# State products in fp32, longer turns and a new order of steps in an attention and softplus kernel on one Trainium2 core

## The chip, the core and the metric

The kernel runs on one core of a Trainium2 chip. Five engines work side by side, each through a queue of its own in order: PE (matrix products, with its weight loads PEld), DVE and ACT (element-wise work; both can read PSUM, where the products land), POOL (element-wise work, in SBUF alone) and SP (issues DMA transfers here). The metric is the device time of one execution in microseconds. The profiled execution has a span, from its first to its last instruction; the time is a little longer than the span.

## The reference

Attention runs both ways between 512 tokens and 32 state rows of each head; then every row of both results goes through a two-layer network with softplus.

```
B, H, S, Ns, D = (8, 8, 512, 32, 64);  d_model, d_ff = 512, 2048
scores  = scale * x @ state^T;  a  = softmax over the state rows;  xread = a @ state
scores2 = scale * state @ x^T;  a2 = softmax over the tokens;      sread = a2 @ x
x = concatenate([xread, sread], axis=2), heads joined to 512 features
h = x @ w_in;  g = max(h, 0) + log1p(exp(-|h|));  out = g @ w_out
```

The two weight matrices come in as 64-bit floats, x and state as 32-bit ones. Products on PE run in one of two ways. An fp32 product takes both operands whole. A split product has its operands as two parts, high and low (F32R), and runs as passes high-high, high-low, low-high.

## The kernel before

**What is computed.** For the token rows, `xread @ w_in` is not done as two products: V = state . w_in is made per head once, and the first layer is `a @ V`. A slot is 128 hidden features of one batch: six products on L454 (`gemm1`), then the softplus on ACT (L438 to L440) and DVE (L441), the split of its result (`ghi` by ACT or POOL, `glo` by DVE or POOL, L85 to L93), and twelve products on L461 (`gemm2`) into four PSUM banks called acc, one for each 128 tokens. There are 16 slots for each of the eight batches, and eight slots of 256 features for the rows of the state read. The banks are: h, two; aux, two; acc, four.

**Stages.** A string of letters sets the order. START covers the whole attention of batches 0 to 2 and the slots of batches 0 and 1; BLOCK runs once for each of the batches 2 to 6; then come the state read and LAST with batch 7. The letters: `|` a slot's first product and softplus, `g` the second product of the oldest slot that waits, `a b c` a step of a batch's attention, `v V U` a step of making V, `W` one 128-row piece of w_out, `F` and `p` the fetch and the split of a piece of V. The set MOVED says which splits and copies go to POOL or DVE.

**Making V.** A 128-row piece of w_in is loaded (`load_w`, L98) and converted from 64 bits to 32 (`as_f32`): an ACT or POOL product with 2^-112 (L114, L112) and three DVE instructions (L124, L125, L126). Six of the pieces take another way (L118 to L122, two DVE instructions and one each on ACT and POOL). The first 512 hidden features (chunk 0, `make_v0`) use fp32 products with the padded state, `QZ` (L167 for batches 0 and 1, kept in SBUF as `vf`; L176 for batches 2 and 3, sent to DRAM). For chunks 1 to 3 `make_v` splits each piece again by head: `head` (L213 to L219) makes the 64 rows of one head into a high and a low half, in the tile `zhl`; `product` (L202 to L211) multiplies them by the state of four batches, `StK`, which lies in the room of two w_out tiles; the result goes through `ve` to DRAM (`Vd`) and comes back by `fetch_v` (L260) for each batch. Batches 4 to 7 are made likewise during the BLOCKs from weights kept in DRAM (`wsc`), in the tile `R`.

**Turns.** Batches 0 and 1 take turns by quarters of the hidden features, eight turns of four slots. At a turn's end the four acc banks go to SBUF: the first time by ACT copies (L549), later by DVE additions (L552).

**Rows of a group** in PE's order: `QZ` and `zhl` stand for the fp32 state products' weights, `zhl,wout` for a head's split products. Two products of 64 columns on L424 end batch 2's attention; the second of them is the last step of START on PE.

Of the kernel before, what the change touches and what calls it, by code (L numbers as in the profile page):

```python
# [12 lines left out]
I64 = mybir.dt.int64  # L13
AF = mybir.ActivationFunctionType
# [5 lines left out]
P = 128  # L20
# [12 lines left out]
RTAGS = ('zhl',)  # L33
VLAG = (2, 2)
V_ORDER = (1, 2, 3)
LOADS = (('t', 0), ('w', 0), ('w', 0), ('w', 0), ('z', 0), ('x', 0), ('q', 1), ('q', 0), ('w', 0), ('w', 0), ('w', 0), ('t', 1), ('w', 0), ('x', 1), ('w', 0))
ATT = (('Q0', 'A0', 'M0', 'Q1', 'N0', 'A1', 'M1', 'D0', 'E0', 'N1', 'E1', 'D1', 'G0', 'R0', 'G1', 'R1', 'X0', 'X1'), ('Q0', 'A0', 'M0', 'N0', 'Q1', 'D0', 'A1', 'M1', 'N1', 'D1', 'E0', 'G0', 'R0', 'X0', 'E1', 'G1', 'R1', 'X1'), ('Y0', 'S0', 'Q0', 'E0', 'A0', 'G0', 'M0', 'N0', 'D0', 'S1', 'R0', 'X0', 'Q1', 'A1', 'E1', 'M1', 'N1', 'G1', 'Y1', 'R1', 'D1', 'X1'), ('S0', 'Q0', 'E0', 'Y0', 'G0', 'A0', 'S1', 'R0', 'M0', 'X0', 'Y1', 'N0', 'Q1', 'A1', 'M1', 'E1', 'G1', 'N1', 'R1', 'X1', 'D1', 'D0'))
START = 'aaagvavavaBavaaavaaaaaaapabvWaWva|vVVVVVbWbV|pbVb|bVbbVbgbgW|VVVgpbb|V|VVbpgVVWbV|bWgbF|gWVWVpbbg|gVp|gVVVV||FgbVpVVV||VVWgVgWVpVVV|WVVg|gVFVWVVggp|V|VVVVVVpggF|gCVp|cg||WgpFcWgpWWcpF||gg|c||cF|cgcccgcpgcpc|g|cccccc|gg|cpcccgc'
BLOCK = 'UBUg|UU|gbpUU|bbgbbU|Fgpbbp|UbUgUbbFU|gUFU|bbUbFbgb|pU|gpbUgUbb|UUUgbpUUgUUp||UUUgUbbpbg|U|gUUU|gb|g'
LAST = 'pFg||gpF|Fggg||pgp|gg||gp|pg||ggg|gp|g|g||'  # L40
# [648 lines left out]
```

## Time and profile before

| | |
|---|---|
| time, median of 3 runs | 726.08 us (726.03 to 726.4) |
| span of the profiled execution | 723.7 us |
| PE busy | 669.6 us |
| DVE busy | 526.1 us |
| ACT busy | 484.9 us |
| POOL busy | 217.2 us |
| data moved | 89.76 MB |

Busy times of PE overlap: a product's record runs from its start to its end, and the next one starts before that end. The stretch between two starts is what a product costs when they follow each other. An fp32 product shows as two records in the trace, and as one row in the order of instructions.

### The profile page before, as it was taken

To read this page: it belongs to the slowest core of one execution; us is meant where nothing else is said; L and a number is where in the kernel's file an instruction comes from. 1 tells how busy PE (TensorE), PEld (TensorE's weight loads), DVE (VectorE), ACT (ScalarE), POOL (GpSimd) and SP (SyncE) were. 2 spreads that over 40 slices of the span, in tenths; PEclk is the share of its full clock that TensorE was granted. 3 is DMA by queue.
4 is the path that set the end of the run, shared out by engine and by line. 5 is a ranking of instruction groups with operands and counts; after the bars stand their busy time and mean duration, and the time that the engine had idled before them with its cause. 6 is when DMAs were issued, how large, how long until landed. Compare 5 with 4: busy or idle time off the path is not lost.

```text
span 723.7 us, 9466 instructions
## 1 busy us (share of the span) xinstructions
PE 669.6 (93%) x3012; PEld 538.4 (74%) x3012; DVE 526.1 (73%) x881; ACT 484.9 (67%) x897; POOL 217.2 (30%) x218
## 2 busy tenths in 40 slices
PE   3777869799799999999999999999999999999997
PEld 1445657577687787887888888888888889988886
DVE  4889888999999999569874975498558744534322
ACT  3565868576767787778786776667666676656653
POOL 2456466645754421022110411141113101012100
PEclk9999999999999999999999999999999999999999
DMA  8777727565632645436442421141112112522001
GB/s 293 232 230 246 242 92 257 171 211 163 191 95 95 209 140 178 124 102 203 153 131 88 145 59 59 30 146 30 29 30 87 30 30 73 161 87 60 1 0 59
DMA packets 46194, 89.76 MB, mean 124 GB/s; under 512 B 6976, under 2 KB 13888, under 8 KB 46144
## 3 DMA queue, kind: packets, MB, share of 16 engines
q1 hardware_dynamic: 46144, 89.15, 38.7%
q8 instruction: 24, 0.39, 0.2%
q14 instruction: 26, 0.21, 0.1%
HBM read 60.29 MB, written 28.84 MB: 123 GB/s over the span
## 4 chain that ended last, share of the span: by engine, by line
PE 56%; DVE 26%; ACT 5%; issue 5%; DMA 2%; POOL 2%; SPq 0%; DVEq 0%; ACTq 0%; POOLq 0%
PE acc L461 33%; PE h L454 15%; PE h L501 3%; DVE t L441 3%; DVE glo L93 2%; DVE k L93 2%; PE aux L204 2%; DVE zhl L219 2%; DVE wt L126 2%; DVE k L125 2%; DVE vhl L93 2%; DVE k L124 1%; DVE k L328 1%; PE aux L387 1%; ACT t L438 1%
## 5 line engine op out<-in xcount | busy, mean ns | idle before, releaser
L461 PE MATMUL acc<-wout,ghi 128*128 128x512 f32 x1088 | 339.7, 393 | 3.5 <-DVE o L144 1.0
L461 PEld LDWEIGHTS acc<-wout,ghi 128*128 128x128 f32 x1088 | 203.0, 189 | 48.1 <-DVE o L144 2.0
L461 PE MATMUL acc<-wout,glo 128*128 128x512 f32 x544 | 212.4, 391 | 0.8 <-DVE glo L93 0.8
L454 PE MATMUL h<-aT,vhl 128*128 128x512 f32 x768 | 198.4, 397 | 12.2 <-DVE t L441 9.7
L454 PEld LDWEIGHTS h<-aT,vhl 128*128 128x128 f32 x768 | 144.1, 190 | 46.1 <-DVE t L441 9.8
L441 DVE SCALAR_TENSOR_TENSOR t<-h,t 128x512 f32<-128x512 f32 x136 | 93.2, 686 | 91.9 <-ACT t L440 91.2
L438 ACT ACTIVATE t<-h 128x512 f32<-128x512 f32 x136 | 80.8, 595 | 90.6 <-PE h L454 80.0
L461 PEld LDWEIGHTS acc<-wout,glo 128*128 128x128 f32 x544 | 102.5, 188 | 23.1 <-DVE glo L93 1.4
L93 DVE TENSOR_TENSOR glo<-t,ghi 128x512 fp32r<-128x512 f32 x98 | 75.0, 765 | 36.1 <-ACT ghi L92 21.0
L85 POOL TENSOR_SCALAR ghi<-t 128x512 fp32r<-128x512 f32 x51 | 34.5, 676 | 221.8 <-DVE t L441 189.9
L440 ACT ACTIVATE t<-t 128x512 f32<-128x512 f32 x136 | 85.6, 631 | 2.4
L439 ACT ACTIVATE t<-t 128x512 f32<-128x512 f32 x136 | 85.7, 632 | 1.4
L92 ACT CAST ghi<-t 128x512 fp32r<-128x512 f32 x85 | 52.7, 620 | 48.3 <-DVE t L441 37.4
L93 POOL TENSOR_TENSOR glo<-t,ghi 128x512 fp32r<-128x512 f32 x38 | 51.5, 1357 | 103.1 <-ACT ghi L92 93.1
L93 DVE TENSOR_TENSOR vhl<-vf,vhl 128x512 fp32r<-128x512 f32 x70 | 55.3, 792 | 29.7 <-ACT vhl L92 29.2
L92 ACT CAST vhl<-vf 128x512 fp32r<-128x512 f32 x69 | 42.2, 613 | 13.9 <-PE h L501 8.6
L209 ACT COPY ve<-aux 128x512 f32<-128x512 f32 x41 | 23.2, 579 | 3.5 <-PE aux L204 1.9
L204 PE MATMUL aux<-zhl,wout 128*128 128x512 f32 x48 | 16.1, 420 | 10.0 <-DVE ve L207 4.1
L501 PEld LDWEIGHTS h<-sreadT,vhl 128*128 128x128 f32 x192 | 24.1, 191 | 0.6
L501 PE MATMUL h<-sreadT,vhl 128*128 128x256 f32 x192 | 24.3, 283 | 0.0
L219 DVE TENSOR_TENSOR R<-wt,R 64x512 fp32r<-64x512 f32 x32 | 22.5, 704 | 2.4 <-ACT R L218 1.4
L126 DVE SCALAR_TENSOR_TENSOR wt<-k,k 128x512 int32<-128x512 int32 (+1 forms) x30 | 21.9, 730 | 2.2 <-POOL wout L93 1.2
(139 smaller groups left out, 745.9 us busy)
## 6 DMA issues: line engine op xcount, KB each, us to landing
vd<-ve SPq DMA_DIRECT2D x56, 256.0 KB, 2.3
vf<-vd SPq DMA_DIRECT2D x112, 128.0 KB, 2.8
xT<-in_xt_dram SPq DMA_DIRECT2D x16, 512.0 KB, 4.5
x<-in_xn_dram SPq DMA_DIRECT2D x16, 512.0 KB, 3.9
k<-in_w_out_dram SPq DMA_DIRECT2D x16, 512.0 KB, 3.8
k<-in_w_in_dram SPq DMA_DIRECT2D x12, 512.0 KB, 4.3
out_dram<-o SPq DMA_DIRECT2D x24, 256.0 KB, 2.1
wt<-wsc SPq DMA_DIRECT2D x16, 256.0 KB, 3.1
```

The source lines that it names most:

```text
L85: nc.gpsimd.tensor_scalar(dst, src, 1.0, 0.0, ALU.mult, ALU.add)
L92: nc.scalar.copy(hi, src)
L93: vec(*what).tensor_tensor(lo, src, f32(hi), ALU.subtract)
L126: nc.vector.scalar_tensor_tensor(r.bitcast(I32), h2.bitcast(I32), 3, u, ALU.logical_shift_left, ALU.bitwise_or)
L219: vec("R", *what, o).tensor_tensor(r[z], wf[a], f32(r[a]), ALU.subtract)
L438: nc.scalar.activation(t, h, AF.Abs)
L439: nc.scalar.activation(t, t, AF.Exp, scale=-1.0)
L440: nc.scalar.activation(t, t, AF.Ln, bias=1.0)
L441: nc.vector.scalar_tensor_tensor(t, h, 0.0, t, ALU.max, ALU.add)
L454: nc.tensor.matmul(h, Vhl[b, ft // 2][:, vi, g, cs], aT[b][:, ai, g], start=(n == 0), stop=(n == 5))
L461: nc.tensor.matmul(acc[c], g[gi][:, c0:c0 + P], wout[ft][:, wi], start=(ft == first and i == 0), stop=(ft == last and i == 2))
L501: nc.tensor.matmul(h[:, 256 * i:256 * i + 256], Whl[u, i][:, wi, kt, :], sreadT[:, si, kt, :], start=(n == 0), stop=(n == 11))
```

## The change

It does the following.

- Chunks 1 to 3 of V for batches 0 to 3 are made as chunk 0 is (`make_vf` in place of `make_v` for the first four batches): two fp32 products of a whole 128-row piece, 128x512, in place of two heads of two split products each. The first product's two halves are copied to SBUF as V of batches 0 and 1, in the room of the w_out tiles 10, 11, 13 and 14 (chunk 3: `vf`), and are not sent to DRAM; the second product holds batches 2 and 3 and goes to DRAM in one transfer a piece. The head splits, `StK` of the first four batches and 24 fetches fall away.
- Turns: five in place of eight, (batch 0, quarter 0), (1, 0-1), (0, 1-2), (1, 2-3), (0, 3).
- The weights of w_in and w_out can be issued ahead of their conversion, by the new letters `i` and `o`. The first eight pieces of w_in have rooms of their own (`k4`, `R`, `o`). The loads of x move from the batch's load to two steps `L` of its attention.
- The conversion's two DVE instructions on 32-bit words (mask the sign, shift and merge) become two on 16-bit halves, which write every second half word; the third stays. All pieces take this way, and its first product is always on ACT.
- START and LAST are new, BLOCK becomes three strings, and MOVED is new: 175 instructions on POOL, where there were 223.

```diff
-        nc.vector.tensor_scalar(u, hi, SIGN, None, ALU.bitwise_and)
-        nc.vector.scalar_tensor_tensor(u, lo, 29, u, ALU.logical_shift_right, ALU.bitwise_or)
+        uh = u.bitcast(U16).rearrange("p (n t) -> p n t", t=2)
+        nc.vector.tensor_scalar(uh[:, :, 0], vh[:, :, 1], 13, None, ALU.logical_shift_right)
+        nc.vector.tensor_scalar(uh[:, :, 1], vh[:, :, 3], 0x8000, None, ALU.bitwise_and)
...
+    VTAGS = {1: ("wout10", "wout11"), 2: ("wout13", "wout14"), 3: ("vf", "vf")}
...
+    def load_ahead(k):
+        if coming[k]:
+            come[k].append(load_w(coming[k].pop(0)))
...
+    def make_vf(cs):
+        for c in cs:
+            for b in range(2):
+                Vf[b, c] = sb(VTAGS[c][b], [P, 2, 512], bufs=2 if c == 3 else 1)
+            for q in range(4):
+                wf = as_f32(ahead("in"), c, q, tag="wout12" if (4 * c + q) % 3 == 2 else "wt")
+                nc.sync.dma_start(wsc[c][P * q:P * q + P, :], wf)
...
+                nc.tensor.matmul(pb, QZ[0][:, q, :], wf, start=True, stop=True)
...
+                for b in range(2):
+                    dst, src = Vf[b, c][r, q // 2], pb[64 * b:64 * b + 64]
...
+                nc.tensor.matmul(pb, QZ[1][:, q, :], wf, start=True, stop=True)
...
+                nc.sync.dma_start(Vd[0, c][:, q, :], ve)
...
+            if what == "L":
+                load_x(b, g)
...
-    slots = [(b, ft) for f0 in range(0, NFT, QTR) for b in (0, 1) for ft in range(f0, f0 + QTR)]
+    turns = [(0, 0, 1), (1, 0, 2), (0, 1, 3), (1, 2, 4), (0, 3, 4)]
+    slots = [(b, ft) for b, q0, q1 in turns for ft in range(QTR * q0, QTR * q1)]
...
-        run(BLOCK, b)
+        run({2: BLOCK2, 3: BLOCK3}.get(b, BLOCK), b)
```

On PE, in START, where a piece of chunk 1 is multiplied (`acc` rows are second products, `h` rows first products, `aux` rows the work on V and attention). Before:

```order
L461 MATMUL acc_555<-wout_130_451,glo_519 128x512
L454 MATMUL h_675<-aT_302,vhl_631 128x512 x3
L204 MATMUL aux_697<-zhl_601,wout_114_411 128x512
L204 MATMUL aux_697<-zhl_601,wout_115_412 128x512
L461 MATMUL acc_556<-wout_130_451,ghi_518 128x512 x2
L461 MATMUL acc_556<-wout_130_451,glo_519 128x512
L381 MATMUL aux_703<-x_198,a2T_647 128x256 x4
L204 MATMUL aux_723<-zhl_602,wout_114_411 128x512
L204 MATMUL aux_723<-zhl_602,wout_115_412 128x512
```

In the changed kernel the same place reads as follows (L215 and L226 are the two fp32 products of a piece, L493 and L500 the slots').

```order
L215 MATMUL aux_428<-wt_417,QZ_87 128x512
L500 MATMUL acc_583<-wout_74_283,ghi_387 128x512
L500 MATMUL acc_583<-wout_74_283,glo_388 128x512
L500 MATMUL acc_584<-wout_74_283,ghi_387 128x512 x2
L500 MATMUL acc_584<-wout_74_283,glo_388 128x512
L500 MATMUL acc_585<-wout_74_283,ghi_387 128x512
L226 MATMUL aux_444<-wt_417,wout_2_88 128x512
L493 MATMUL h_544<-aT_113,vhl_471 128x512 x4
L500 MATMUL acc_585<-wout_74_283,ghi_387 128x512
L215 MATMUL aux_462<-wout_133_457,QZ_87 128x512
```

A piece's two heads, of two rows each, have become two rows, whose operand is the converted piece itself, and they stand among the same slots' products.

On DVE, in START, at the conversion of one piece. Before, with the two head splits (L219) that follow it:

```order
L124 TENSOR_SCALAR k_193_669<-k_191_665 128x512
L358 RECIPROCAL rs_774<-rs_774 128x1
L125 SCALAR_TENSOR_TENSOR k_193_669<-k_191_665,k_193_669 128x512
L126 SCALAR_TENSOR_TENSOR wt_670<-k_192_667,k_193_669 128x512
L93 TENSOR_TENSOR wout_166_573<-wt_579,wout_166_573 128x512
L219 TENSOR_TENSOR zhl_691<-wt_670,zhl_691 64x512
L441 SCALAR_TENSOR_TENSOR t_656<-h_649,t_656 128x512
L219 TENSOR_TENSOR zhl_692<-wt_670,zhl_692 64x512
```

In the changed kernel, two conversions (a piece of w_in, `k_118`, and one of w_out, `k_126`), in START after the first softplus:

```order
L127 TENSOR_SCALAR k_118_416<-k_107_391 128x512
L129 SCALAR_TENSOR_TENSOR wt_398<-k_109_395,k_110_397 128x256
L128 TENSOR_SCALAR k_118_416<-k_107_391 128x512
L127 TENSOR_SCALAR k_126_437<-k_90_328 128x512
L129 SCALAR_TENSOR_TENSOR wt_417<-k_117_414,k_118_416 128x512
L128 TENSOR_SCALAR k_126_437<-k_90_328 128x512
L380 TENSOR_REDUCE sm_449<-T_393 128x16
```

One of the two instructions with two inputs has become one with a single input, and no split stands between the conversion and the product of `wt_417`.

On SP, at the start of the program, the loads in the order of their issue. Before:

```order
L274 DMA xT_90<-in_xt_dram 128x1024
L98 DMA k_4_92<-in_w_in_dram 128x256
L98 DMA k_5_94<-in_w_in_dram 128x256
L98 DMA k_6_96<-in_w_in_dram 128x256
L286 DMA Z_73<-in_zp_dram 128x2x64 x2
L279 DMA x_100<-in_xn_dram 128x1024
L616 DMA zhl_89<-in_zq_dram 128x512
L616 DMA QZ_88<-in_zq_dram 128x512
```

In the changed kernel:

```order
L310 DMA xT_89<-in_xt_dram 128x1024
L322 DMA Z_73<-in_zp_dram 128x2x64 x2
L98 DMA k_4_93<-in_w_in_dram 128x256
L98 DMA k_5_95<-in_w_in_dram 128x256
L310 DMA xT_97<-in_xt_dram 128x1024
L98 DMA k_7_99<-in_w_in_dram 128x256
L98 DMA k_8_101<-in_w_in_dram 128x256
L98 DMA R_103<-in_w_in_dram 128x256
```

The scores' operands (xT, Z) of both groups now stand ahead of most weights, and x has left this place; it is issued after the first three writes to `wsc`.

## Rows read from the trace of the kernel before

**Rows 1.** The page: busy time by engine, and the span in 40 slices.

```profile
PE 669.6 (93%) x3012; PEld 538.4 (74%) x3012; DVE 526.1 (73%) x881; ACT 484.9 (67%) x897; POOL 217.2 (30%) x218
...
PE   3777869799799999999999999999999999999997
...
DVE  4889888999999999569874975498558744534322
```

**Rows 2.** Windows: busy us (and records) by engine, granted clock, DMA share, GB/s.

```profile
0.00:40.00 40.00, 21.66 (x69) 13.26 (x69) 27.95 (x65) 16.85 (x40) 15.02 (x24) 0.93 0.80 260
40.00:229.50 189.50, 161.69 (x673) 122.97 (x671) 174.14 (x259) 129.88 (x245) 108.47 (x95) 0.98 0.56 182
229.50:310.00 80.50, 78.52 (x352) 63.25 (x352) 67.73 (x119) 64.74 (x120) 19.95 (x19) 1.00 0.50 159
310.00:390.00 80.00, 78.93 (x357) 64.21 (x356) 63.88 (x110) 62.98 (x116) 15.66 (x17) 1.00 0.45 143
390.00:461.00 71.00, 70.68 (x323) 58.15 (x323) 48.73 (x89) 49.08 (x90) 15.32 (x17) 1.00 0.27 79
```

**Rows 3.** Waits of PE, 40 to 229.5 us: total, times, longest.

```profile
PE h L454 <- DVE t L441: 9.7, 4, 3.9
PE aux L204 <- DVE ve L207: 4.1, 4, 1.6
PE aux L204 <- POOL zhl L219: 2.6, 4, 0.8
PE aux L204 <- DVE zhl L219: 1.6, 2, 0.8
```

**Rows 4.** Timeline of PE: start, duration; first slot, fp32 products, START's last step.

```profile
30.04 1.89 PE L381 MATMUL acc<-x,a2T 128*128 128x256 f32 x8
...
39.91 2.48 PE L454 MATMUL h<-aT,vhl 128*128 128x512 f32 x6
...
51.50 1.88 PE L317 MATMUL aux<-xT,Z 128*128 128x512 f32 x4
...
229.45 0.27 PE L424 MATMUL aux<-ident,sr 64*128 64x64 f32 x1
```

**Rows 5.** The chain of waits, one of its pieces: start, us, twelve products.

```profile
294.98 2.72 PE acc L461 x12
```

**Rows 6.** Groups of 0 to 229.5 us: busy us, mean ns, idle before.

```profile
L125 DVE SCALAR_TENSOR_TENSOR k<-k,k 128x512 int32<-128x512 int32 x24 | 19.8, 826 | 0.3
L126 DVE SCALAR_TENSOR_TENSOR wt<-k,k 128x512 int32<-128x512 int32 x24 | 19.5, 811 | 2.2 <-POOL wout L93 1.2 <-issue 0.5 <-DVE k L125 0.2
L219 DVE TENSOR_TENSOR zhl<-wt,zhl 64x512 fp32r<-64x512 f32 x16 | 17.3, 1083 | 2.3 <-ACT zhl L218 1.3 <-POOL zhl L85 0.5
L93 DVE TENSOR_TENSOR glo<-t,ghi 128x512 fp32r<-128x512 f32 x14 | 16.1, 1150 | 1.0 <-POOL ghi L85 0.5 <-ACT ghi L92 0.4
L124 DVE TENSOR_SCALAR k<-k 128x512 int32<-128x512 int32 x24 | 14.8, 617 | 0.1
L552 DVE TENSOR_TENSOR StK<-acc,StK 128x512 f32<-128x512 f32 x12 | 7.8, 673 | 0.0
```

**Rows 7.** Groups of 229.5 to 724 us, the same split later in the program.

```profile
L93 DVE TENSOR_TENSOR glo<-t,ghi 128x512 fp32r<-128x512 f32 x84 | 58.9, 701 | 35.1 <-ACT ghi L92 20.7 <-POOL ghi L85 13.3
```

**Rows 8.** Timeline of DVE and POOL: the same instructions alone and beside POOL.

```profile
31.01 0.42 DVE L124 TENSOR_SCALAR k<-k 128x512 int32<-128x512 int32 x1
...
31.94 0.69 DVE L125 SCALAR_TENSOR_TENSOR k<-k,k 128x512 int32<-128x512 int32 x1
...
100.36 1.64 POOL L93 TENSOR_TENSOR wout<-wt,wout 128x512 fp32r<-128x512 f32 x1
...
100.86 1.42 DVE L124 TENSOR_SCALAR k<-k 128x512 int32<-128x512 int32 x1
```

**Rows 9.** DMA issues: count, size, median us to landing.

```profile
k<-in_w_in_dram SPq DMA_DIRECT2D x12, 512.0 KB, 4.3
```

More of the change, by code (lines that the diff above doesn't have):

```diff
@@ L13 @@
 I64 = mybir.dt.int64
+U16 = mybir.dt.uint16
 AF = mybir.ActivationFunctionType
@@ L163, in make_v0 @@
             for q in range(4):
-                wt = as_f32(first.pop(0), 0, half, q)
+                k = 4 * half + q
+                wt = as_f32(first.pop(0), 0, half, q, tag=f"wout{4 + k}" if k < 6 else "wt")
                 nc.sync.dma_start(wsc[0][P * q:P * q + P, cs], wt)
@@ L181, in make_v0 @@
                     nc.scalar.copy(ve, pb[:, 0:256])
-                nc.sync.dma_start(Vd0[:, q, cs], ve)
+                nc.sync.dma_start(Vd[0, 0][:, q, cs], ve)
                 made["v0", half] = q
                 yield
-    StK = {}
-    def prep_stk(g4, tags):
-        if len(tags) > 1:
-            k = [sb(tag, [P, H, P], F32R) for tag in tags]
-        else:
-            t = sb(tags[0], [P, 2, H, P], F32R)
-            k = [t[:, 0], t[:, 1]]
-        StK[g4] = k
+    coming = {"in": [w_in[c, q] for c in range(1, 4) for q in range(4)],
+              "out": [w_out[P * ft:P * ft + P, :] for ft in range(NFT)]}
@@ new lines, in attention_then_softplus_mlp, with ahead @@
+    come = {"in": [], "out": []}
+    def load_ahead(k):
+        if coming[k]:
+            come[k].append(load_w(coming[k].pop(0)))
+    def ahead(k):
+        if not come[k]:
+            load_ahead(k)
+        return come[k].pop(0)
+    def make_vf(cs):
[5 more added lines that the diff above has]
+                nc.sync.dma_start(wsc[c][P * q:P * q + P, :], wf)
+                yield
+                pb = aux()
+                nc.tensor.matmul(pb, QZ[0][:, q, :], wf, start=True, stop=True)
+                r = slice(64 * (q % 2), 64 * (q % 2) + 64)
+                for b in range(2):
+                    dst, src = Vf[b, c][r, q // 2], pb[64 * b:64 * b + 64]
+                    if ("vd", c, q, b) in MOVED:
+                        nc.vector.tensor_copy(dst, src)
+                    else:
+                        nc.scalar.copy(dst, src)
+                made["v", c] = q
+                yield
+                pb = aux()
+                nc.tensor.matmul(pb, QZ[1][:, q, :], wf, start=True, stop=True)
+                ve = sb("ve", [P, 512], bufs=2)
+                if ("ve", 0, c, 2 * q + 1) in MOVED:
+                    nc.vector.tensor_copy(ve, pb)
+                else:
+                    nc.scalar.copy(ve, pb)
+                nc.sync.dma_start(Vd[0, c][:, q, :], ve)
+                made[0, c] = q
+                yield
@@ L430, in split_wout @@
     def split_wout(ft):
-        assert ft < NFT - 2 or all(made[0, c] == H for c in range(1, 4))
+        assert ft < NFT - 1 or all(made[0, c] == 3 for c in range(1, 4))
         wout[ft] = sb(f"wout{ft}", [P, 2, DM], F32R)
-        w = as_f32(load_w(w_out[P * ft:P * ft + P, :]), ft)
+        w = as_f32(ahead("out"), ft)
         split(wout[ft][:, 0], wout[ft][:, 1], w, "wout", ft)
@@ L455, in gemm1 @@
                 n += 1
-        return softplus(h, b, ft)
+        return softplus(h, min(b, 4), ft)
     def gemm2(acc, g, ft, cols, first=0, last=NFT - 1):
@@ L531, in flush @@
             return
-        first = ft // QTR * QTR if b < 2 else 0
-        last = first + QTR - 1 if b < 2 else NFT - 1
+        first, last = next(r for r in runs.get(b, [(0, NFT - 1)]) if r[0] <= ft <= r[1])
         if ft == first:
@@ L554, in flush @@
                     nc.sync.dma_start(d, p)
-    fetches = [(fetch_w, (ft,)) if b == B else (fetch_v, (b, ft // 4)) for b, ft in slots if b == B or ft % 4 == 0][2:]
+    fetches = [(fetch_w, (ft,)) if b == B else (fetch_v, (b, ft // 4)) for b, ft in slots if b == B or ft % 4 == 0 and b > 1]
     pieces = [(split_w, (ft,)) if b == B else (split_v, (b, ft // 2)) for b, ft in slots if b == B or ft % 2 == 0]
-    wt_tags = [f"wout{NFT - 2 + i}" for i in range(2)]
     first = []
@@ L597, in run @@
                     break
+            elif what in "io":
+                load_ahead({"i": "in", "o": "out"}[what])
             elif what == "g":
@@ L618, in attention_then_softplus_mlp @@
             load_z(0)
-        elif what == "t":
+        else:
             load_xT(0, i)
-        else:
-            load_x(0, i)
     run(START)
```

100 lines of the change are left out of this document (47 added, 53 removed).

## The prediction

> **What bounds the kernel now.** I read the page first. PE is busy for 93% of the span, and its slices fall below 9 nearly only in the first third; DVE is at 8 or 9 in just these slices and at 3 to 7 later [rows 1]. So the program has two parts, and the timeline gives their border: START ends on PE at 229.5 us [rows 4].
>
> Behind it, PE is the bound. Twelve split products in a row take 2.72 us, 0.227 each [rows 5]. With that price, half of it for the 256-wide ones, and the fp32 prices below, the products behind START sum to 477.8 us of the 494.2 us left, 97%.
>
> In START it is otherwise. The products there sum to 164.1 us of 229.5, so 65.4 us are lost: about 22 before the first slot at 39.9 us [rows 4], where 18.2 us of products stand, and 43 after it. The window from 40 us on shows PE "busy" for 161.7 of 189.5 us, but the products are worth only 145.9, or 77%, while DVE is busy for 174.1, or 92% [rows 2]. The waits agree: PE's longest is for DVE's last softplus instruction, then come evacuations and head splits [rows 3]. These named waits are 18.0 us; the other 25 lie in gaps that no wait holds. The clock was granted at 0.98 there and 0.93 before [rows 2], so it explains little. START is bound by DVE, and by whatever makes DVE's instructions long.
>
> Three windows give a scale. With DVE at 92% PE's products fill 77%; with DVE at 84% (229.5 to 310 us) they fill 95%; at 80% (310 to 390 us), 97% [rows 2]. I interpolate on it: 2.25 points of PE for one of DVE between 84% and 92%.
>
> **The change part by part.**
>
> *PE.* 48 split products of V (10.9 us) leave START and 24 fp32 ones of 512 columns come. Two such products, four records, take 1.88 us with the last one's tail [rows 4], so 0.87 each, 20.9 us; four of 256 columns take 1.89, 0.43 each, which agrees. That is +10.0. By the order nine more slots' products stand ahead of START's end: +2.0 there, −2.0 behind. START's products become 176.1 us, the rest's 475.8.
>
> *DVE, busy in START 202.1 us* (27.95 and 174.14 [rows 2]). Head splits: 16 of 1.083 go, one of 0.7 comes: −16.6 [rows 6, 7]. Turns: 20 additions in START become 8, at 0.673: −8.1 [rows 6]. Conversion: 24 pieces cost 14.8 + 19.8 + 19.5 = 54.1 [rows 6], four more take another way with two instructions of about 0.69, together 59.6. Now all 28 have two halves and the merge. The halves' form is nowhere in this trace. As the masking instruction runs alone, a half is 0.42 and the merge about 0.69 [rows 8]: 1.53, in all 42.8. As the rows of START are stretched, 0.617 twice and 0.811 [rows 6]: 57.3. If a half is no better than the two-input instruction that it replaces, 0.826 [rows 6], 2.46 a piece: 69. A gain is not certain, then; I take 1.8 a piece, 50, since the nearest row is the one-input instruction on the same words: −9.6. The 256-wide pieces I leave as they are. Against this, splits come from POOL to DVE: by the order five of w_out, four of g and two of a, eleven at about 0.8, +8.8. The other state splits and small steps: −2.8; copies out of PSUM: +1.5. The sum is −26.8, so 175.3 us.
>
> *POOL.* It falls from 123.5 us [rows 2] to 55 instructions, some 61 us at 1.4 for two inputs and 0.75 for one. This matters to DVE, not by itself: beside a two-input POOL instruction of 1.64 us, a DVE instruction of 0.42 took 1.42 [rows 8], and `glo` means 1.150 in START against 0.701 later [rows 6, 7]. By such differences about 30 us of DVE in START are stretch. My prices above hold half of the relief; another 7 to 10 us would be the whole.
>
> *ACT.* Casts for the heads (−15) and evacuations (−11) go; copies of 64 rows, casts of w_out and the conversion's first product come: +4.4 us in all. ACT is busy 129.9 of 189.5 us [rows 2], and that room hides it; without the room it costs up to 4. One place is nearer to the path: the first fp32 product's bank is freed only by two copies, and aux has two banks, so PE's products on V can wait there; the 4.1 us of `ve` waits [rows 3] are what such waits cost now, and I leave them in.
>
> *SP.* Fifty fewer DMAs stand in START, and the loads of weights come earlier. A load issued ahead waits for the last readers (ACT, DVE) of its `k4` room; queued behind it are writes to `wsc`, which free the converted piece for DVE's next merge, and writes of V, which free `ve` for the next evacuation. Such a stall costs 0 to one landing, 4.3 us [rows 9], each. I take 0: no row of PE's waits in START names a DMA [rows 3], and the DMA share was 0.56 [rows 2]. V of batches 0 and 1 now sits in rooms of w_out tiles, so those tiles' splits wait for its last reader; 0 to 2 us, taken 0, because they come at START's end, when few pieces are left to convert. The x loads move behind the operands of the scores, but still ahead of their use: 0 to 2, taken 0.
>
> *First slot.* DVE's work ahead of the first softplus falls from 30.8 to 24.9 us by the order and the clean prices [rows 8], and the operands of the scores are issued earlier. DVE is busy for 28 of the first 40 us [rows 2], so I move the first slot from 39.9 to 36, with 16.5 us of products ahead of it and 24.9 us of DVE.
>
> *Sum.* After the first slot START has 176.1 − 16.5 = 159.6 us of products and 175.3 − 24.9 = 150.4 us of DVE. If it lasts 175.3 us, DVE is at 86%, the scale gives PE 91%, and 159.6/0.91 is 175.3 again. START ends at 211.3. Behind it 494.2 − 2.0 = 492.2, nothing else taken off (a part of the 4 us that PE lacks from 229.5 to 310 us could go). The span is 703.5; the median lies 2.4 us over the span of 723.7 us: **706 us**.
>
> **The rivals.**
>
> *DVE goes free (bigger gain).* If the stretch goes altogether and the conversion costs 1.53, DVE falls to about 158, 133 us after the first slot. PE then fills 97%, as at 310 to 390 us [rows 2]: 36 + 159.6/0.97 = 200.5, so 695 us. For it: POOL halves. Against it: half of POOL's instructions stay, and DVE was not alone in the later windows either.
>
> *The halves are slow (smaller gain).* 16-bit words written at every second place may not stream as 32-bit words do. Priced as above, 0.83 a half and 0.75 for the merge, 28 pieces cost 67.5 in place of 50, and the 16 pieces of 256 columns some 4 more: DVE has 196. At 92%, as now [rows 2], 171/0.92 = 186 us after the first slot, START ends at 222, and the time is 716.5. For it: no row shows such a write. Against it: the masking instruction reads every second 32-bit word and still takes 0.42 us for 512 [rows 8].
>
> [...]
>
> *The fp32 products are paid in full (slower).* If START's losses are not DVE's but the order's, the 25 us in unnamed gaps and the filling at the start, then PE's +12.0 land in full and only the waits on head splits, 4.2 us [rows 3], go: START ends at 237, and the time is 732. It decides from a START end of 231.5 us, that is if fewer than 10 of the 65.4 lost us are won. For it: each product holds PE for 0.87 us between slots whose softplus waits. Against it: DVE at 92% [rows 2] loses 27 us of work, more than twice what PE gains.
>
> *No difference*: START ends near 231.5, since about 10 us are won and 12 added.
>
> **How the numbers follow.** The forecast, 0.57, is 698 to 714, from the conversion's bounds and the waits taken at 0. DVE free has 0.14, slow halves 0.14, slower 0.11, no difference 0.04. Faster is 0.57 + 0.14 + 0.14 = 0.85. 0.2%, 1.5 us, is about what a measurement of this kernel can tell from no change. The range, 692 to 722, leaves out the slower case, no difference, and the lower end of DVE free, together 0.18.
>
> **What would show it.** The second 64-column product of the state read ends START at 211 us (200 to 222 for the two gains, 237 for slower). The first slot starts near 36. The halves' rows mean 0.42 to 0.6 us; 0.8 or more means that they are slow. DVE's busy sum to START's end is 175 and POOL's 61; `glo` means under 1 us there. PE's waits for DVE's softplus fall below 9.7 us. The fp32 products are two records of 0.43 apart. Behind START 492 us remain. The forecast is wrong if PE in START waits for DMA (a stalled SP), if DVE's sum falls and PE's idle time does not, or if BLOCK's windows grow.

## The result: 717.8 us, 1.1% faster, where 706 was forecast

The changed kernel takes 717.8 us (median of 4 runs, 717.45 to 718.53) against 726.06 for the kernel before on the same chip. The ratio is 0.9890, with a 95% interval of 0.9876 to 0.9904. So it is faster, by 8.3 us and not by 20. The profiled execution has a span of 715.7 us, 2.1 us under the median. START ends at 218.8 us (211.3 forecast, 229.5 before [rows 4]), and 496.9 us lie behind it (492.2 forecast, 494.2 before).

The page of the changed kernel, busy time by engine and the span in 40 slices, to be held against [rows 1]:

```profile
PE 685.2 (96%) x3012; PEld 537.2 (75%) x3012; DVE 474.8 (66%) x854; ACT 502.4 (70%) x914; POOL 174.5 (24%) x170
...
PE   5679899999999999999999999999999999999997
...
DVE  4499788855799998688758773777377634544322
```

PE is at 9 from the sixth slice to the last but one, where before it fell below 9 again and again in the first eleven. DVE has lost its long run of 8 and 9. What is left of PE's loss stands at the left edge.

The windows of the changed kernel, cut at 37 us (first slot), at 60 us and at START's end; the columns are those of [rows 2]:

```profile
0.00:37.00 37.00, 22.88 (x65) 13.39 (x66) 15.99 (x46) 15.33 (x34) 7.29 (x12) 0.91 0.74 248
37.00:60.00 23.00, 17.33 (x53) 10.29 (x53) 22.45 (x48) 18.73 (x38) 5.16 (x5) 0.85 0.75 246
60.00:218.80 158.80, 154.47 (x633) 115.34 (x631) 121.78 (x222) 118.35 (x220) 51.33 (x47) 0.99 0.44 147
218.80:715.70 496.90, 490.52 (x2266) 398.21 (x2265) 314.57 (x541) 349.96 (x624) 110.74 (x106) 1.00 0.29 90
```

DVE's sum to START's end is 16.0 + 22.5 + 121.8 = 160.2 us (175.3 forecast, 202.1 before), POOL's 63.8 (61 forecast). In the window from 37 to 60 us DVE is busy for 98% and PE for far less; from 60 us on it is the other way round.

To say how much PE lost, I count the products by their records and price each as in the prediction (0.227 us a split product of 512 columns, 0.87 an fp32 one, 0.43 an fp32 one of 256). A transpose of 128 columns counts 0.09, an estimate of mine by which the prediction's 477.8 us behind START come out; at 36.5 us of the changed kernel one record of a transpose lasts 0.27 us and four in a row 0.60, so they start 0.11 apart. Lost time is the time that has passed less the products begun by then:

| by | before: products, lost | after: products, lost |
|---|---|---|
| first slot (39.9, 36.9 us) | 15.8, 24.1 | 14.9, 22.0 |
| 60 us | 29.3, 30.7 | 28.3, 31.7 |
| START's end (229.5, 218.8 us) | 163.7, 65.7 | 175.8, 43.0 |

Up to 60 us the change won nothing. Between there and START's end PE lost 35.0 us before and 11.3 after: the whole gain. It is nearly 24 us, of which 12 pay for the products that START has more of: 10 for the dearer ones, 2 for slots' products that now stand ahead of its end.

Where the start was lost: PE's waits in the first 60 us of the changed kernel (total, times, longest; the wait for Z stands at the very start of the program), and then DVE's and SP's timelines (start, duration, instruction, and in brackets the idle time before it).

```profile
PE aux L356 <- DMA Z<-in_zp_dram: 5.1, 1, 5.1
PE h L493 <- DVE sreadT L92: 5.1, 1, 5.1
...
PE aux L356 <- DMA xT<-in_xt_dram: 2.3, 2, 1.5
```

```profile
36.70 0.72 DVE L370 STREAM_TRANSPOSE T<-aux 128x512 f32<-128x512 f32 x1 [7.83 <-PE aux L356]
37.34 0.42 DVE L127 TENSOR_SCALAR k<-k 128x512 uint16<-128x512 uint16 x1
...
43.19 0.23 DVE L92 TENSOR_TENSOR sreadT<-h,sreadT 64x64 fp32r<-64x64 f32 x1
```

```profile
24.37 1.21 SPq L322 DMA_DIRECT2D Z<-in_zp_dram  x2
27.14 0.33 SPq L188 DMA_DIRECT2D vd<-ve  x1
27.52 0.42 SPq L310 DMA_DIRECT2D xT<-in_xt_dram  x1
...
28.49 0.48 SPq L310 DMA_DIRECT2D xT<-in_xt_dram  x1
```

Read from below. SP issues the load of batch 1's xT at 27.5 us, behind a write of V that waits for its evacuation. PE has batch 1's scores (L356) ahead of the first slot and waits 1.5 us for that load; the second of the two score products then stands behind batch 0's state read (L420). DVE has the transpose of these scores (L370) ahead of three conversions and of the four splits of batch 0's state read (`sreadT`), and stands still for 7.8 us. Then everything falls due at once: the last of the four splits is done at 43.4 us, and only then is the bank free in which the second slot's products are to land. Of PE:

```profile
32.98 1.10 PE L356 MATMUL aux<-xT,Z 128*128 128x512 f32 x2 [1.54 <-DMA xT<-in_xt_dram]
...
35.64 1.02 PE L356 MATMUL aux<-xT,Z 128*128 128x512 f32 x2
...
36.85 1.64 PE L493 MATMUL h<-aT,vhl 128*128 128x512 f32 x6
43.56 0.77 PE L493 MATMUL h<-aT,vhl 128*128 128x512 f32 x1 [5.07 <-DVE sreadT L92]
```

The first slot came at 36.85 us, as forecast (36); the second came 6.7 us behind it.

Three of the runs below have the changed kernel's order up to here: the one with the old order behind START, the one with eight turns and the one with more products. In their traces DVE waits 10.0 to 10.2 us at the same place and PE 5.1, their first slots come at 38.8 to 39.7 us, and 33.3 to 34.0 us are lost by 60 us, where it is 31.7 here. So the wait belongs to the order, and two executions of one order differ by some 2 us in the time lost by 60 us. Of the run with the old order behind START, on DVE:

```profile
39.05 0.72 DVE L370 STREAM_TRANSPOSE T<-aux 128x512 f32<-128x512 f32 x1 [10.02 <-PE aux L356]
```

### The profile page after: what moved, and what is told of

It reads as the page before. It is cut to its first block, busy times and chain, and to the rows that moved or that the text cites. A ratio compares the mean times of both kernels' runs of the same rounds, so it can differ in the third digit from the quotient of the medians.

```text
span 715.7 us, 9243 instructions
## 1 busy us (share of the span) xinstructions
PE 685.2 (96%) x3012; PEld 537.2 (75%) x3012; DVE 474.8 (66%) x854; ACT 502.4 (70%) x914; POOL 174.5 (24%) x170
## 3 DMA queue, kind: packets, MB, share of 16 engines
q1 hardware_dynamic: 42016, 82.33, 35.5%
## 4 chain that ended last, share of the span: by engine, by line
PE 71%; ACT 9%; DVE 8%; DMA 5%; issue 3%; POOL 3%; SPq 0%; DVEq 0%; POOLq 0%; ACTq 0%
PE acc L500 42%; PE h L493 19%; PE h L540 3%; DMA k<-in_w_in_dram 2%; PE aux L250 1%; ACT t L478 1%; ACT t L479 1%; DVE t L480 1%; ACT t L477 1%; PE aux L426 1%; PE aux L362 1%; DMA wout<-in_zq_dram 1%; ACT ghi L91 1%; POOL glo L92 1%; DMA xT<-in_xt_dram 1%
## 5 line engine op out<-in xcount | busy, mean ns | idle before, releaser
L500 PE MATMUL acc<-wout,ghi 128*128 128x512 f32 x1088 | 344.4, 394 | 1.2 <-DVE StK L592 0.5
L500 PEld LDWEIGHTS acc<-wout,ghi 128*128 128x128 f32 x1088 | 203.1, 188 | 49.6 <-issue 3.4
L500 PE MATMUL acc<-wout,glo 128*128 128x512 f32 x544 | 215.0, 395 | 0.0
L493 PE MATMUL h<-aT,vhl 128*128 128x512 f32 x768 | 204.2, 402 | 6.5 <-DVE sreadT L92 5.1
L493 PEld LDWEIGHTS h<-aT,vhl 128*128 128x128 f32 x768 | 142.8, 189 | 46.5 <-issue 10.3
L500 PEld LDWEIGHTS acc<-wout,glo 128*128 128x128 f32 x544 | 102.2, 188 | 23.2 <-issue 1.4
L92 DVE TENSOR_TENSOR glo<-t,ghi 128x512 fp32r<-128x512 f32 x100 | 70.3, 703 | 36.0 <-ACT ghi L91 15.6
L91 ACT CAST ghi<-t 128x512 fp32r<-128x512 f32 x104 | 64.5, 621 | 37.0 <-PE acc L500 23.3
L92 DVE TENSOR_TENSOR vhl<-vf,vhl 128x512 fp32r<-128x512 f32 x62 | 46.5, 750 | 35.9 <-ACT vhl L91 33.2
L84 POOL TENSOR_SCALAR ghi<-t 128x512 fp32r<-128x512 f32 x32 | 21.9, 684 | 177.5 <-PE acc L500 137.8
L91 ACT CAST vhl<-vf 128x512 fp32r<-128x512 f32 x59 | 36.4, 616 | 18.1 <-PE h L540 11.7
L383 POOL TENSOR_TENSOR T<-T,sm 128x512 f32<-128x512 f32 x13 | 15.2, 1167 | 119.4 <-DVE sm L382 83.8
L116 ACT ACTIVATE k<-k 128x512 f32<-128x512 f32 (+1 forms) x32 | 20.6, 646 | 9.9 <-DMA k<-in_w_in_dram 8.2
L367 DVE TENSOR_TENSOR k<-aux,k 64x512 f32<-64x512 f32 x24 | 16.4, 683 | 12.5 <-ACT k L366 12.3
L127 DVE TENSOR_SCALAR k<-k 128x512 uint16<-128x512 uint16 (+1 forms) x32 | 16.6, 520 | 7.7 <-DMA k<-in_w_in_dram 7.7
```

The costliest lines, as they stand in the source:

```text
L116: nc.scalar.activation(h2, f32(hi), AF.Copy, scale=2.0 ** -112)
L127: nc.vector.tensor_scalar(uh[:, :, 0], vh[:, :, 1], 13, None, ALU.logical_shift_right)
L493: nc.tensor.matmul(h, Vhl[b, ft // 2][:, vi, g, cs], aT[b][:, ai, g], start=(n == 0), stop=(n == 5))
L500: nc.tensor.matmul(acc[c], g[gi][:, c0:c0 + P], wout[ft][:, wi], start=(ft == first and i == 0), stop=(ft == last and i == 2))
```

## The experiments

Each kernel was timed beside the kernel before; ratios are to that one, with their intervals. The changed kernel has 0.9890 (0.9876 to 0.9904), and 0.001 is 0.7 us. The lost time and the products up to 60 us are counted as above.

### The start: batch 1's scores later, or their operand earlier

The first run takes the score products of batch 1 and the steps behind them later, so that on PE they stand behind the first products of the first two slots (letters of START; b is a step of batch 1's attention):

```diff
-START = 'aavvaaavaaavaavgavaaBoaWaboapbaaobaWvaa|ibvgVbiVoWVbVVV...
+START = 'aavvaaavaaavaavgavaaBoaWaboapbaaoaWvaa|ivgViVoWbVbbVbVV...
```

> The changed kernel with batch 1's score products and the steps after them moved behind the first two slots; all else as it is. Theory A (the fill): the changed kernel lost 8 us of what I forecast before 44 us, because DVE stands in order for 7.8 us before the transpose of batch 1's scores (28.9 to 36.7 us), whose operand is loaded late, and the state read's splits and the conversions behind it hold the second slot's bank (5.1 us wait of PE). Then the first slot starts near 33 us, the second follows without a wait, PE's lost time up to 60 us falls from 32.6 to about 26, and the time is 711 to 714 us, less what batch 1's later attention gives back at its first slot. Rival B (START is paced by loads and conversions, in whatever order): the first slots come earlier but the next ones wait, and the time stays within 1.5 us of 717.8.

715.88 us, 0.9851 (0.9834 to 0.9867). The first slots start at 35.5 and 39.3 us, the lost time by 60 us is 28.4 (31.7). But 33.9 (34.7) is lost by 80 us: batch 1's slots now wait for what was put off. By the ratios 2.8 us less than the changed kernel, by the medians 1.9: in A's direction, and short of its 711 to 714.

The second run issues the loads (B) fourteen letters earlier:

```diff
-START = 'aavvaaavaaavaavgavaaBoaWaboapbaaobaWvaa|...
+START = 'aavvaaBavaaavaavgavaaoaWaboapbaaobaWvaa|...
```

> The changed kernel with batch 1's loads of xT and Z issued after the third step of DVE work (behind two writes to wsc) in place of behind six writes of V; order of steps otherwise as it is; the loads of batch 0's x come some places later for it. Theory A: DVE's wait of 7.8 us before the transpose of batch 1's scores falls under 3 us, the second slot starts 4 to 6 us earlier, and the time is 712 to 715 us. Rival B: what the loads win at one place they lose at another (x of batch 0 comes late and PE waits for it), and the time stays within 1.5 us of 717.8.

714.23 us, 0.9825 (0.9810 to 0.9839): 4.7 us under the changed kernel by the ratios, 3.6 by the medians. SP now issues the two loads at 17.3 and 18.8 us; on DVE the transpose of batch 1's scores runs without a wait, and the window from 37 to 60 us has fewer instructions on DVE and more on PE. Of this run, SP's and DVE's timelines and that window:

```profile
17.33 0.42 SPq L310 DMA_DIRECT2D xT<-in_xt_dram  x1
...
18.83 0.42 SPq L310 DMA_DIRECT2D xT<-in_xt_dram  x1
```

```profile
29.85 0.71 DVE L370 STREAM_TRANSPOSE T<-aux 128x512 f32<-128x512 f32 x1
```

```profile
37.00:60.00 23.00, 19.17 (x60) 12.18 (x59) 16.92 (x36) 18.20 (x39) 4.45 (x5) 0.85 0.77 255
```

DVE moved 5.5 us of work from that window into its former idle time. The first slot starts at 36.9 us as before, the second at 40.7 in place of 43.6. PE has begun 30.7 us of products by 60 us, in place of 28.3: 2.4 more, hardly more than two executions of one order differ by. START ends at 216.0 us, 2.8 earlier, and the profiled span is 2.9 shorter. What shows the gain is the times, whose intervals lie apart. So theory A holds for this part of the miss: the late load of one tile, which I had put down at nothing.

Two runs join both edits. The first also has one letter `a` more ahead of `vg` (`...vaaavgavaa...`), by which the later steps of batch 0's attention come one place earlier; the second has the loads only a little earlier (`...vaaBvgavaaoa...` in place of `...vvaaBavaaa...`):

> The changed kernel with both edits of the fill: batch 1's loads of xT and Z issued earlier, and batch 1's score products and following steps behind the first two slots. Theory A (the fill holds 8 us of my miss): if the two edits remove different waits, 712 to 714 us; if they remove the same one, no better than the early loads alone, 713.5 to 715. Rival B (what the fill gains is taken back when batch 1's slots begin at 60 us): 714 to 717.

> As the run with both edits of the fill, but with batch 1's loads only four places earlier than in the changed kernel, behind the loads of batch 0's x. Theory A: 712 to 715 us; the second product of the state read does not wait for x, and batch 1's scores do not wait for xT. Rival B: 714 to 717, as the gain is taken back when batch 1's slots begin.

716.16 us, 0.9865 (0.9833 to 0.9897), and 715.13 us, 0.9841 (0.9826 to 0.9855). Neither beats the early loads alone: the edits remove the same wait, and in all three traces PE's wait for `sreadT` is 2.2 us. By 80 us 35.3 and 33.5 are lost, where the early loads alone have lost 33.5: what the first slots gain is taken back, as B had it.

The last one has the early loads, the one letter `a` more, and takes the first slot ahead of the end of batch 0's attention, which it does not need (against the changed kernel):

```diff
-START = 'aavvaaavaaavaavgavaaBoaWaboapbaaobaWvaa|ibvg...
+START = 'aavvaaBavaaavaaavgavaaoaWaboap|baaobaWvaaibvg...
```

> The changed kernel with batch 1's early loads, and with the first slot taken ahead of the last steps of batch 0's attention (both products of its state read, batch 1's scores), which it does not need. Theory A (the order of the fill sets the first slot): the first slot starts at 27 to 30 us in place of 36.9, PE's lost time up to 60 us falls from 32.6 to 24 to 27, and the time is 710 to 713.5 us. Rival B (the fill is paced by loads and conversions): the first products come earlier, but the first second products still start at 44 to 48 us, since w_out's first piece is loaded no earlier, and the time is no better than with the early loads alone, 714 or more.

715.31 us, 0.9831 (0.9807 to 0.9856). PE's timeline of this run:

```profile
28.07 3.17 PE L493 MATMUL h<-aT,vhl 128*128 128x512 f32 x10
...
39.31 0.96 PE L500 MATMUL acc<-wout,ghi 128*128 128x512 f32 x3 [1.04 <-POOL wout L84]
...
51.44 1.19 PE L173 MATMUL aux<-wt,QZ 128*128 128x256 f32 x2 [3.49 <-DVE sreadT L92]
...
57.51 2.27 PE L493 MATMUL h<-aT,vhl 128*128 128x512 f32 x3
```

The first slot starts at 28.1 us and the second products at 39.3, so the loads did not hold them, as B said they would. At 50 us 26.1 us are lost, the fewest of all; at 60 us it is 32.4 again, and the time is B's. The third slot needs the second half of chunk 0 of V, whose products (L173) come at 44 to 53 us behind DVE's queue, so it starts at 57.5. In the traces of the six orders of the start, the changed kernel's among them, 28 to 32 us are lost by 60 us. What they share there is DVE's list (conversions of the last pieces of chunk 0, the state read's splits, batch 1's softmax). They share the loads as well: in each trace the DMA engines move 14.8 to 15.4 MB in the first 60 us and are busy for 74 to 80% of them. Which of the two sets the floor is not shown: no run took work off the one or bytes off the other in this stretch alone.

### DVE: conversion and turns, undone and added

The conversion on 32-bit words again:

```diff
-        nc.vector.tensor_scalar(uh[:, :, 0], vh[:, :, 1], 13, None, ALU.logical_shift_right)
-        nc.vector.tensor_scalar(uh[:, :, 1], vh[:, :, 3], 0x8000, None, ALU.bitwise_and)
+        nc.vector.tensor_scalar(u, hi, SIGN, None, ALU.bitwise_and)
+        nc.vector.scalar_tensor_tensor(u, lo, 29, u, ALU.logical_shift_right, ALU.bitwise_or)
```

> The changed kernel with the conversion's two instructions on 32-bit words, as before, in place of those on 16-bit halves. The halves mean 0.54 us each in START of the changed kernel; the 32-bit ones should be 0.45 to 0.6 and 0.7 to 0.8 with POOL as light as it is, so DVE gets 4 to 9 us more to do in START. Theory A (after 44 us PE is the bound, DVE being busy for 79%): under 1.5 us slower. Rival C (START is still bound by DVE): 4 to 9 us slower.

719.54 us, 0.9901 (0.9886 to 0.9916): 0.8 us over the changed kernel by the ratio, 1.7 by the medians, and the intervals overlap. C's 4 to 9 us are out.

Eight turns again:

```diff
-    turns = [(0, 0, 1), (1, 0, 2), (0, 1, 3), (1, 2, 4), (0, 3, 4)]
+    turns = [(b, q, q + 1) for q in range(4) for b in (0, 1)]
```

> The changed kernel with eight turns of four slots for batches 0 and 1, as before: 12 additions of 0.68 us more on DVE, 8.2 us, most of them in START, and three more ends of turns at which PE's banks must be emptied. Theory A (PE is the bound after 44 us): 0 to 2 us slower, from the banks' ends alone. Rival C (DVE is the bound): 5 to 8 us slower.

722.43 us, 0.9937 (0.9916 to 0.9958): 3.4 us more by the ratio, 4.6 by the medians, between the two expectations. In the profiled execution 2.3 us are lost by 60 us, before any addition is due and with the order as it was, which is no more than two executions of one order differ by. So the turns cost 3.4 to 4.6 us at most, and how much of it is theirs stays open.

The second half of every conversion written twice:

```diff
+        nc.vector.tensor_scalar(uh[:, :, 1], vh[:, :, 3], 0x8000, None, ALU.bitwise_and)
```

> The changed kernel with the second 16-bit half of every conversion written twice: 28 instructions of 0.53 us and 16 of 0.3 us, 18 us more of DVE, 15 of them after 44 us, where DVE then is busy for 87% in place of 79%. Theory A (PE is the bound there, DVE has room): under 4 us slower. Rival C (DVE is the bound): 12 to 18 us slower.

721.61 us, 0.9937 (0.9913 to 0.9961). The added copies cost DVE 12.8 us for 28 of 512 columns and 2.7 for the narrow ones; the time grows by 3.4 us, a fifth to a quarter of that. A's bound of 4 holds, C's 12 to 18 are out.

### PE: more products

Each fp32 product for batches 0 and 1 made twice (the line is repeated):

```diff
+                nc.tensor.matmul(pb, QZ[0][:, q, :], wf, start=True, stop=True)
```

> The changed kernel with each of the twelve 128x512 fp32 products for batches 0 and 1 made twice into the same bank: 12 products at 0.87 us, 10.4 us more of PE in START. Theory A (after 44 us PE is the bound): 8 to 11 us slower. Rival C (DVE is the bound and PE has room, 10% of it): under 4 us slower. If an fp32 product costs less than the 0.87 us I took, the slowdown is smaller, and the records' distance shows it.

727.06 us, 1.0004 (0.9991 to 1.0016): 8.3 us more by the ratio, 9.3 by the medians, for 10.4 us of products. The price was right, by this run's timeline (the two products of the pair, then the one of batches 2 and 3):

```profile
111.59 1.02 PE L215 MATMUL aux<-wout,QZ 128*128 128x512 f32 x2
112.46 1.02 PE L216 MATMUL aux<-wout,QZ 128*128 128x512 f32 x2
113.31 1.02 PE L227 MATMUL aux<-wout,wout 128*128 128x512 f32 x2
```

They stand 0.87 and 0.85 us apart. So in START of the changed kernel PE work is paid at 80 to 90% and DVE work at a quarter: PE is the bound there, from about 50 us on, where the added products stand. By this run's rate the fp32 products' 10 us were paid nearly in full, as the slower rival had it; what paid for them is that PE stopped losing time between products.

### The conversion alone, in the kernel before

The same lines as in the changed kernel, in the kernel before:

```diff
-        nc.vector.tensor_scalar(u, hi, SIGN, None, ALU.bitwise_and)
-        nc.vector.scalar_tensor_tensor(u, lo, 29, u, ALU.logical_shift_right, ALU.bitwise_or)
+        nc.vector.tensor_scalar(uh[:, :, 0], vh[:, :, 1], 13, None, ALU.logical_shift_right)
+        nc.vector.tensor_scalar(uh[:, :, 1], vh[:, :, 3], 0x8000, None, ALU.bitwise_and)
```

> The kernel before with the conversion on 16-bit halves alone; the order of steps, turns and products of before. In its START the two instructions on 32-bit words mean 0.617 and 0.826 us (24 pieces); the halves, one input each, should be 0.5 to 0.6 each, so DVE gets 8 to 11 us less to do. If START of before is bound by DVE, as I held, it passes on: START ends 5 to 9 us earlier, 717 to 721 us. If it is bound by its order and waits (rival), the time falls by less than 3 us.

727.54 us, 1.0005 (0.9990 to 1.0019): nothing. Two things were wrong with my expectation. Its groups of the first 229.5 us (busy us, mean ns, idle before) and the window of [rows 2]:

```profile
L129 DVE SCALAR_TENSOR_TENSOR wt<-k,k 128x512 int32<-128x512 int32 x24 | 19.7, 819 | 2.2 <-POOL zhl L222 1.0 <-DVE k L128 0.2
L128 DVE TENSOR_SCALAR k<-k 128x512 uint16<-128x512 uint16 x24 | 18.3, 761 | 0.0
L127 DVE TENSOR_SCALAR k<-k 128x512 uint16<-128x512 uint16 x24 | 15.3, 639 | 0.0
```

```profile
40.00:229.50 189.50, 161.54 (x674) 123.56 (x672) 168.88 (x257) 130.66 (x244) 105.43 (x95) 0.98 0.57 183
```

The halves take 0.639 and 0.761 us there, hardly less than the 32-bit words (0.617 and 0.826 [rows 6]). And the 5.3 us that DVE does save in this window change nothing: "DVE 92% busy, so DVE is the bound" was too short. DVE's queue was full, but PE waited for single results in it: 6.9 us for the softplus even here (9.7 before [rows 3]). That these waits came from the order is my reading; no run shows it by itself. In the changed kernel the same two instructions mean less (groups up to 220 us):

```profile
L129 DVE SCALAR_TENSOR_TENSOR wt<-k,k 128x512 int32<-128x512 int32 x24 | 17.5, 730 | 3.6 <-PE aux L226 2.6 <-ACT k L116 0.5 <-DVE k L128 0.2
L127 DVE TENSOR_SCALAR k<-k 128x512 uint16<-128x512 uint16 x28 | 15.5, 552 | 0.0
L128 DVE TENSOR_SCALAR k<-k 128x512 uint16<-128x512 uint16 x28 | 14.9, 531 | 0.0
L92 DVE TENSOR_TENSOR glo<-t,ghi 128x512 fp32r<-128x512 f32 x18 | 12.4, 691 | 4.2 <-ACT ghi L91 3.3 <-POOL ghi L84 0.9
```

### POOL as busy as before

37 entries that the kernel before had in MOVED are put back into that of the changed one: 18 subtractions (of `g` 9, `wout` 5, `v` 2, `at` 2) and 19 casts, such as `('g', 0, 3)` and `('hi', 'v', 0, 0)`.

> The changed kernel with 37 casts and subtractions of START (of w_out, of V, of a, of the softplus results) put on POOL, where the kernel before had them: 14 two-input ones leave DVE (some 10 us), 23 casts leave ACT, and POOL is about as busy in START as before, some 100 us. Theory F (a DVE instruction is stretched beside POOL, the 16-bit halves too; the conversion alone gained nothing in the kernel before for this reason): the halves mean 0.62 to 0.75 us in START in place of 0.54, the merge 0.80 or more, DVE's busy sum falls by less than 5 us though it has 10 us less to do, and the time is 1 to 5 us longer because of the slower chains. Rival G (the halves were slow in that run for another reason, such as their place in the order): they stay at 0.54 and DVE's sum falls by 8 to 12 us.

723.13 us, 0.9948 (0.9932 to 0.9964): 4.2 us more. Its groups and windows:

```profile
L129 DVE SCALAR_TENSOR_TENSOR wt<-k,k 128x512 int32<-128x512 int32 x24 | 22.2, 924 | 4.7 <-POOL wout L92 2.1 <-ACT k L116 1.6 <-ACT t L477 0.6
...
L128 DVE TENSOR_SCALAR k<-k 128x512 uint16<-128x512 uint16 x28 | 18.5, 661 | 0.0
L127 DVE TENSOR_SCALAR k<-k 128x512 uint16<-128x512 uint16 x28 | 17.2, 615 | 1.6 <-DMA k<-in_w_out_dram 1.5
```

```profile
0.00:44.00 44.00, 25.94 (x76) 15.42 (x76) 25.01 (x62) 18.71 (x43) 11.69 (x17) 0.86 0.73 245
44.00:218.80 174.80, 165.03 (x655) 120.74 (x656) 133.78 (x227) 123.64 (x229) 84.63 (x82) 0.98 0.48 157
```

Of the 37 entries 18 are instructions with two inputs (my expectation counted 14), so DVE has some 12 us less to do, at 0.69 each. Yet it is busy for 25.0 + 133.8 = 158.8 us, 1.4 less than in the changed kernel: the halves are busy for 5.3 us more and the merge for 4.7, and they took most of the difference. Theory F holds. How it comes about shows in DVE's and POOL's timelines of the changed kernel:

```profile
121.23 0.51 DVE L127 TENSOR_SCALAR k<-k 128x512 uint16<-128x512 uint16 x1
121.64 1.53 DVE L128 TENSOR_SCALAR k<-k 128x512 uint16<-128x512 uint16 x1
123.07 0.44 DVE L127 TENSOR_SCALAR k<-k 128x512 uint16<-128x512 uint16 x1
```

```profile
121.51 1.35 POOL L92 TENSOR_TENSOR glo<-t,ghi 128x512 fp32r<-128x512 f32 x1
```

A half is 0.44 us by itself. The one that comes while POOL subtracts two tiles is 1.53 us, and ends 0.3 us behind POOL, as if it stood still and then ran. POOL had started 0.13 us earlier. In START of the changed kernel the four halves that begin while POOL is in an instruction with two inputs took 1.53 to 1.56 us, and each ends 0.31 to 0.33 behind that instruction; the six others that overlap an instruction of POOL took 0.45 to 0.89. Why the four take so long no run shows.

### The order behind START

The blocks and LAST of the changed kernel get the strings of the kernel before (with the two new steps `bb` behind each B):

```diff
-BLOCK = 'gBbUUp|UU|bUb||gUUUbFU...
+BLOCK = 'UBbbUg|UU|gbpUU|bbgbbU|Fg...
```

> The changed kernel with the order of the kernel before in the five blocks and in LAST (START and everything else of the changed kernel). The stretch behind START is 496.9 us in the changed kernel, 494.2 before, with the same products or fewer; its blocks last 71.9 us where they lasted 71.1 to 71.4. Theory D (the new order behind START costs this): the stretch shrinks by 2 to 4 us, the time is 714 to 716. Rival E (it is the products themselves, or work that START left undone): within 1.5 us of 717.8, or slower where the old order doesn't fit the new placing of work.

720.35 us, 0.9908 (0.9890 to 0.9925): not faster, 1.3 us slower by the ratio with overlapping intervals. The stretch behind START is 498.1 us. Theory D is not borne out; the old order does not fit the new placing of work either, so this run does not show what the new order costs by itself. By PE's waits the changed kernel has 1.7 us of them behind START, the kernel before 3.8, this run 7.4. What the new order gives back shows in the products' own records, 330 to 570 us (busy us, mean ns), first before, then after:

```profile
L461 PE MATMUL acc<-wout,ghi 128*128 128x512 f32 x420 | 130.0, 391 | 1.0 <-DVE o L144 1.0
...
L454 PE MATMUL h<-aT,vhl 128*128 128x512 f32 x312 | 78.5, 392 | 0.0
```

```profile
L500 PE MATMUL acc<-wout,ghi 128*128 128x512 f32 x420 | 132.3, 393 | 0.2
...
L493 PE MATMUL h<-aT,vhl 128*128 128x512 f32 x312 | 79.8, 394 | 0.3
```

The records are 2 ns longer each, with hardly a wait between them. Records overlap, so the distance of their starts says what this costs. Behind START, 512-wide split products that follow each other within 240 ns are 228.5 ns apart on average, where it was 227.3: 2.1 us over 1865 of them. 76 more stand further apart (42 before) and lose 10.7 us in place of 7.2. Why stays open: part of it follows the order (392 ns on both lines with the old blocks), and no run here took it apart.

## Why the prediction went wrong, step by step

- **The direction and what paid.** Faster, as forecast, and within the range. PE's losses in START fell by 22.7 us, the fp32 products cost about 10, as priced.
- **The step that failed: the scale, taken from the first slot on.** I let PE fill 91% from the first slot (36 us, met) to START's end. That gives 16.5 + 24 x 0.91 = 38.3 us of products by 60 us; it was 28.3. This is 10.0 us of the miss of 12. Of these, 1.6 are products that I counted ahead of the first slot and that do not stand there (14.9, not 16.5; before 15.8, not 18.2); the others were lost from the first slot to 60 us, where PE filled 58%. The row to read was there: by 60 us the kernel before had begun 29.3 us of products, and from 39.9 to 60 us it filled 67%. I averaged that into the 77% of 40 to 229.5 us [rows 2], and then carried the scale of full stages over to a stage that is filling.
- **SP and the x and xT loads, taken at 0.** The early loads gave 3.6 to 4.7 us back, so this term was not 0; that it lies near the bound of one landing, 4.3 us [rows 9], is no proof of that bound. My reason, that no row of PE's waits in START named a DMA [rows 3], was a misreading: those rows begin at 40 us, and from 0 to 60 us the same trace has (the first of them at the very start of the program)

```profile
PE aux L317 <- DMA Z<-in_zp_dram: 8.0, 1, 8.0
...
PE aux L317 <- DMA xT<-in_xt_dram: 4.5, 2, 2.7
```

  In the changed kernel, besides, DVE stood behind PE behind the DMA. The order that I had before me showed the transpose of batch 1's scores ahead of the conversions on DVE; I did not ask who would wait for it. The sign that I had named, PE in START waiting for a DMA, came true with 1.5 us on PE, and it cost DVE 7.8.
- **The unnamed gaps.** I set 18.0 us of PE's waits from 40 us on against 25 us in gaps that no wait holds. The 18.0 are the four longest rows alone; all rows of that window are 27.5 us, so some 14 are left for the gaps, of the 42 us lost there.
- **From 60 us on.** 147.5 us of products took 158.8 us, 92.9%; by the forecast's 91% 2.2 us more would have been lost. But it came near for the wrong reason: DVE was at 77% there, where my scale gives 97% or more. The runs with more DVE work and more PE work show why the scale does not hold: PE pays 80 to 90% of what is added to it, and DVE a quarter.
- **DVE's sum.** 160.2 us where I had 175.3, nearly the 158 of the rival "DVE goes free". The conversion is as priced (0.55, 0.53 and 0.73 us, 1.81 a piece). The rest of the stretch went with POOL's work: `glo` means 0.691 in START, where it was 1.150 and I had kept half of the difference [rows 6, 7]. That rival's mechanism came true and its 695 us did not, because DVE was not what PE lacked.
- **The halves** are not slow by themselves: 0.42 to 0.47 us with a write at every second half word, away from POOL's instructions. Beside one with two inputs they took 1.53 to 1.56 (four cases). That 716.5 us, the time of this rival, lies near the result is chance.
- **The slower rival.** Its premise came true (PE's added work is paid). It missed the price of the losses: 22.7 of the 65.7 us were won, where it needed fewer than 10.
- **START's products** were 175.8 us (176.1 forecast), and 475.8 stand behind it, as forecast.
- **Behind START** 496.9 us in place of 492.2. The products are not the cause: 21.1 us are lost between them, where it was 16.4 before. I had no term for these 4.7 us, and their cause stays open.

The sum, lost time against the forecast's: 10.0 by 60 us − 2.2 from there to START's end − 0.3 of products + 4.7 behind START = 12.2 us, and the span is 715.7 where I had 703.5. Of these the late load explains 3.6 to 4.7 by the times of its run; the rest of the filling's loss is measured, and its cause is open (DVE's list or the loads).

What also stays open: how the nearly 24 us won between 60 us and START's end divide among the head splits that went (products no longer wait for `zhl`) and the new order. Undone alone, the conversion gives back about 1 us, within the noise, the turns 3.4 to 4.6 at most and POOL's load 4; undoing the products in the new order wasn't tried, since START of the one does not fit the other.

## What to carry to other kernels

Before a share of busy time is used as a scale, cut the window where the pipeline is still filling: here PE filled 67% of the stretch from the first slot to 60 us before the change and 58% after it, and from 60 us to START's end 79 and 93%. When the order of instructions is at hand, look for the first instruction on each engine that needs a late load, and list what stands behind it; a load that shows as 1.5 us in PE's waits held another engine for 7.8 us here. And read a list of waits whole, from the first microsecond, before saying what is not in it. Test which engine is paid for by adding a little work to each: two runs said more than all the shares.

## What the runs showed of the hardware

- A 16-bit instruction with one input that reads every fourth half word and writes every second (512 of them) took 0.42 to 0.47 us on DVE in all 46 cases in START that no POOL instruction overlaps, about as long as the one on 32-bit words at every second place, 0.42 [rows 8]. The four that began while POOL was in an instruction with two inputs took 1.53 to 1.56.
- In the changed kernel PE stood idle from 38.5 to 43.6 us, the 5.07 us ahead of the second slot. The granted clock was 0.51 from 44 to 48 us and 1.00 from 48 to 52. Windows:

```profile
44.00:48.00 4.00, 3.96 (x10) 2.73 (x10) 4.00 (x10) 2.95 (x6) 0.00 (x0) 0.51 0.75 241
48.00:52.00 4.00, 4.00 (x17) 2.72 (x16) 3.84 (x10) 3.77 (x8) 1.81 (x2) 1.00 0.93 317
```

  PE has ten records in the first 4 us and 17 in the next; by these counts the first stretch did the work of some 2.4 us and cost some 1.6, an estimate. With the early loads PE stood idle for 2.2 and 0.9 us there, and the granted clock of the same 4 us was 0.50, so it is no part of their gain. What sets the clock no run shows. Of the run with the early loads:

```profile
44.00:48.00 4.00, 4.00 (x11) 3.06 (x11) 3.37 (x9) 3.30 (x8) 0.00 (x0) 0.50 0.31 104
```
